# A ranking product ten places behind its logits, and the first expert's gathers three places later

## The chip, the core and the metric

One core of a Trainium2 chip runs the whole program. The metric is the device time of one execution in microseconds (us). TensorE (PE) multiplies matrices, VectorE (DVE) and ScalarE (ACT) work on tiles, GpSimd (POOL) issues the indirect transfers (scatters and gathers by a list of rows), and SyncE (SP) issues the plain transfers. Each engine works through a queue of its own in order, and an instruction that has to wait holds up everything behind it on that engine.

## What is computed

Attention over 4 sequences of 576 tokens with 8 heads and fixed masks; then a gated feed-forward layer; then a mixture of 8 experts of which each token uses two. The core of the reference, with what matters here:

```python
attn = softmax(where(mask, q @ k.T / sqrt(D), -1e9)); x = attn @ v       # 2304 tokens x 512
x = (x @ w_a) * (x @ w_b) @ w_out                                        # 512 -> 1536 -> 512
noisy = x @ w_gate + log1p(exp(x @ w_noise)) * noise                     # 2304 x 8
top2 = argpartition(-noisy, 2, axis=1)[:, :2]
top2_w = exp(l - max(l)) / (sum + 1e-9)                                  # l: the two chosen logits
for e in range(8):
    for k in range(2):
        mask = top2[:, k] == e
        out[mask] += top2_w[mask, k] * (relu(x[mask] @ w1[e]) @ w2[e])
```

## The kernel before

Full-precision products are made of three matmuls on split operands (a high part `...h` and a low part `...l`; the helper is L196 to L198). The feed-forward layer runs over five chunks of tokens: chunks 0 to 3 have 512 tokens each (the first 512 of a sequence), chunk 4 has the 256 tokens that are left. A chunk takes twelve steps f = 0 to 11 of 128 hidden units. A step makes `pa` and `pb` (stage_a), `a` on ACT (L703), the product `a*pb` on DVE (L708), its parts `gh` (ACT, L709) and `gl` (DVE, L710). The products into `po` (stage_b) are made one step later: in step f PE runs `pa` and `pb` of f and then `po` of f - 1. In chunk 4, `pa` and `pb` of one step are 24 matmuls of 256 columns, `po` is 6 of 512 columns.

When a chunk's `po` is complete, its routing follows in the next chunk's steps, in pieces: `finish` is a generator, and each `yield` in it ends a piece. Twice per stage_a and once per stage_b a step calls `point()`, which lets the routing go on by one piece, and the loading of expert weights by one or two. For the fourth chunk (c = 3) the pieces run in chunk 4 from f = 1 on: four times a transposition of 128 rows and their logits (eight pieces), then the routing proper on DVE and ACT (L451 to L478), which ends in `ms`, the two chosen experts of each token as ones and zeros. Some empty pieces later PE makes the ranking product (L485): fourteen small matmuls that count, for each token and expert, the tokens before it. From it DVE makes `sli`, the slot of each token in its expert's list (L491 to L498), and POOL scatters the tokens' numbers and weights into the table in DRAM (L510, eight scatters for a chunk of 512).

The first expert's tokens are fetched during chunk 4's last steps by the generator `first` = fetch(0, [0, 1, 2]): load the table (L757, on SP), gather 128 rows (L763, on POOL) twice, transpose the first of the two on PE (L772) and evacuate it into `x00h`, `x00l`, gather the third, transpose the others. A place in the table that chunk 4 fills begins only behind these three tiles, so they depend on the scatters of chunks 0 to 3 alone. The step at which each `next(first)` stands fixes its place on PE; two gathers may be open at a time.

The expert weights come meanwhile through two stage buffers `st` of 512 KB (L156, on SP), one half of a 1 MB unit each; ACT and DVE convert each half into the high and low part (L159, L160: `w0h`, `w0l` to `w7h`, `w7l`, two conversions of each for a half). A buffer is free for the next load when its conversions are done. Units 0 to 2 and 3 to 5 lie where the feed-forward weights of f = 0 to 3 and f = 4 to 7 were, so they can be converted only after chunk 4 has used those for the last time.

PE's order is the order in which the program is written. The order of the other engines is set by a scheduler when the program is built, from estimated times; it can change around the change, though the code there is the same.

Of the kernel before, what the change touches and what calls it, by code (L numbers as in the profile page):

```python
# [32 lines left out]
def attention_moe_kernel(ctx: ExitStack, tc: tile.TileContext, q, k, v, w_a, w_b, w_out,  # L33
                         w_gate, w_noise, noise, w1, w2, out):
    nc = tc.nc
    B, H, S, D = q.shape
    DM = H * D
    DFF = w_a.shape[1]
    E, _, FE = w1.shape
    CT = 512  # L40
    TL = S - CT
    NCH = B + 1
# [157 lines left out]
    def pt(shape, name="tt"):  # L200
        return psum.tile(shape, F32, name=name, tag="t", bufs=2)
# [219 lines left out]
    def tile_of(c):  # L421

        return (4 * c, 4) if c < B else (4 * B, TL * B // 128)
# [22 lines left out]
    def route(c, lg):  # L446
        T0, J = tile_of(c)
        z = lg[:, :, 8:16]
        t4 = rpool.tile([128, 4, J, 8], F32, name="t4", tag="t4")
        e, w, r, sp = (t4[:, i] for i in range(4))  # L450
        nc.vector.tensor_scalar(r, z, -1.0, None, op0=OP.mult)  # L451
        nc.vector.tensor_tensor(r, r, z, op=OP.max)
        nc.scalar.activation(e, r, AF.Exp, scale=-1.0)
        nc.vector.tensor_scalar(w, e, 1.0, None, op0=OP.add)
        nc.scalar.activation(sp, w, AF.Ln)
        nc.vector.scalar_tensor_tensor(e, w, -1.0, e, op0=OP.add, op1=OP.subtract)
        nc.vector.reciprocal(r, w)
        nc.vector.tensor_mul(e, e, r)
        nc.vector.tensor_sub(sp, sp, e)
        nc.vector.scalar_tensor_tensor(sp, z, 0.0, sp, op0=OP.max, op1=OP.add)  # L460
        nc.vector.tensor_mul(sp, sp, noise_sb[:, T0:T0 + J, :])
        nc.vector.tensor_add(sp, sp, lg[:, :, 0:8])
        m8 = rpool.tile([128, J, 8], F32, name="m8", tag="m8")
        i8 = rpool.tile([128, J, 8], U32, name="i8", tag="i8")
        for j in range(J):
            nc.vector.max(m8[:, j, :], sp[:, j, :])
            nc.vector.max_index(i8[:, j, :], m8[:, j, :], sp[:, j, :])
        wt = rpool.tile([128, 2, J], F32, name="wt", tag="wt")
        nc.vector.tensor_sub(wt[:, 1, :], m8[:, :, 1], m8[:, :, 0])
        nc.scalar.activation(wt[:, 1, :], wt[:, 1, :], AF.Exp)  # L470
        idf = rpool.tile([128, J, 2], F32, name="idf", tag="idf")
        nc.vector.tensor_copy(idf, i8[:, :, 0:2])
        oh = rpool.tile([128, J, 2, 8], F32, name="oh", tag="oh")
        for j in range(J):
            nc.vector.tensor_tensor(oh[:, j], iota8[:, None, :].to_broadcast([128, 2, 8]),
                                    idf[:, j, :, None].to_broadcast([128, 2, 8]), op=OP.is_equal)
        ms = rpool.tile([128, J, 8], BF, name="ms", tag="ms")
        nc.vector.tensor_add(ms, oh[:, :, 0, :], oh[:, :, 1, :])  # L478
        yield
        yield  # L480
        yield
        rk = pt([128, J + 1, 8])
        for j in range(J + 1):
            for jj in range(min(j, J - 1) + 1):
                nc.tensor.matmul(rk[:, j, :], tri if jj == j else ones, ms[:, jj, :],  # L485
                                 start=(jj == 0), stop=(jj == min(j, J - 1)))
        if c == NCH - 1:
            for e in range(2):
                nc.vector.tensor_scalar(base[:, e:e + 1], base[:, e:e + 1], float(e * NT + GAP), None, op0=OP.max)
        sl = rpool.tile([128, J, 8], F32, name="sl", tag="sl")  # L490
        nc.vector.tensor_add(sl, rk[:, 0:J, :], base[:, None, :].to_broadcast([128, J, 8]))  # L491
        nc.vector.tensor_add(base, base, rk[:, J, :])
        for kk in range(2):
            nc.vector.tensor_mul(oh[:, :, kk, :], oh[:, :, kk, :], sl)
        slf = rpool.tile([128, 2 * J], F32, name="slf", tag="slf")
        nc.vector.tensor_reduce(slf, oh.rearrange("p j k e -> p (j k) e"), axis=AX.X, op=OP.add)
        sli = rpool.tile([128, 2 * J], I32, name="sli", tag="sli", bufs=2)
        nc.vector.tensor_copy(sli, slf)  # L498
        pay = rpool.tile([128, J, 2, 2], I32, name="pay", tag="pay", bufs=2)
        for kk in range(2):  # L500
            nc.vector.tensor_copy(pay[:, :, kk, 0], ids[:, T0:T0 + J])
        payf = pay.bitcast(F32)
        den = rpool.tile([128, J], F32, name="den", tag="den")
        nc.vector.tensor_scalar(den, wt[:, 1, :], 1.0, 1e-9, op0=OP.add, op1=OP.add)
        nc.vector.reciprocal(den, den)
        nc.vector.tensor_copy(payf[:, :, 0, 1], den)
        nc.vector.tensor_mul(payf[:, :, 1, 1], wt[:, 1, :], den)
        for j in range(J):
            for kk in range(2):
                ins = nc.gpsimd.indirect_dma_start(  # L510
                    out=table, out_offset=bass.IndirectOffsetOnAxis(ap=sli[:, 2 * j + kk:2 * j + kk + 1], axis=0),
                    in_=pay[:, j, kk, :], in_offset=None)
                for o in scatters:
                    tc.declare_no_dep(ins.ins, o.ins, reason="every slot is written once")
                scatters.append(ins)
        yield
# [20 lines left out]
    bgq, attq, finq = [], [], []  # L537

    def advance(queue):
        while queue:  # L540
            try:
                next(queue[0])
                queue.append(queue.pop(0))
                return
            except StopIteration:
                queue.pop(0)
# [5 lines left out]
    def drain():  # L552
        while bgq or finq:
            pump()
# [75 lines left out]
    def conv_to(n):  # L630

        while nconv[0] < n:
            nconv[0] += 1
            if behind[0] is None:
                next(conv)
            else:
                with tc.issue_after(behind[0].ins):
                    next(conv)
# [151 lines left out]
    with tc.manual_schedule(engines={mybir.EngineType.PE}):  # L790
        first = fetch(0, [0, 1, 2])
        prev = None
        npt = [0]
        for c, f in ORDER:
            n0, n1 = nconv[0], min(48, 12 + 3 * (f + 1) if f < 8 else 36 + 6 * (f - 7))

            def point():
                npt[0] += 1
                if c == 0:
                    conv_to(n0 + (n1 - n0) * ((npt[0] - 1) % 3 + 1) // 3)  # L800
                advance(attq)
                advance(finq if finq else attq)
                advance(bgq)
                if c == NCH - 1:
                    advance(bgq)

            if c == 0 and f == 8:
                conv_to(36)
                last_units(cp, 10, ("u0", "u1", "u2"))
                conv_room["raw"] = halves(rpool, [128, 512, 2], "raw", "row")  # L810
                conv_room["ct"] = lambda m: rpool.tile([128, 512], I32, name="ct", tag="x2T")
            if f == NF - 1:
                while c + 1 < B and (c + 1, HPS[-1]) not in attended:
                    advance(attq)
                if c == 0:
                    conv_to(48)
            if c == 1 and f == 0:
                late_setup()
            if (c, f) == (B - 1, 0):
                bgq.append(clear_out())  # L820
                att.close()
                xr = ctx.enter_context(tc.tile_pool(name="xr", bufs=1, side="right"))
                xpool[0, 0] = xr
                xpool["g"] = xr
            if (c, f) == (B - 1, 2):
                for kd in HPS:
                    xf[B, kd] = mpool.tile([128, TL * B], F32, name="xf", tag="xf", bufs=4)
                    nc.sync.dma_start(xf[B, kd], tails[:, kd, :])
            if (c, f) == (NCH - 1, 4):
                bgq.append(load_expert(0))  # L830
            if c == NCH - 1 and f in (8, 11):
                for _ in range(3 if f == 8 else 2):
                    next(first)
            g = stage_a(c, f, point)
            if f == NF - 1 and c + 1 < NCH:
                for kd in HPS:
                    split_kd(c + 1, kd)
                may[0] = c + 2
            if prev is not None:
                rows = stage_b(*prev, point)  # L840
                if rows is not None:
                    finq.append(finish(prev[0], rows))
            prev = (c, f, g)
        drain()
        last_rows = stage_b(*prev, pump)
        for _ in first:
            pass
# [175 lines left out]
```

## Time and profile before

| | |
|---|---|
| median of 3 runs | 1141.54 us (1140.45 to 1141.98) |
| profiled execution | 1142.42 us |
| its span, first to last instruction | 1140.6 us |
| mean granted TensorE clock | 0.961 of 2.4 GHz |
| PE busy | 1097.2 us, 96% |
| DVE, ACT, POOL busy | 511.5, 432.3, 141.8 us |
| longest wait of PE for another engine | 6.9 us, product L485 for `ms` |

The profile tells for each instruction when it started, how long it ran and, where its engine had been idle before it, what ended that wait. PE's matmuls overlap, so the distance from one start to the next tells more than the length of one. The granted clock has two levels, 1.00 (2.4 GHz) and 0.50 (1.2 GHz); a number between them is a mean over a stretch.

### The profile page before, as it was taken

What the parts mean: (1) busy time and instruction counts of PE and PEld (TensorE: products, weight loads), DVE (VectorE), ACT (ScalarE), POOL (GpSimd) and SP (SyncE); (2) the same over time, 40 slices, a digit from 0 to 9 for tenths busy, and PEclk for the clock granted to TensorE, in tenths of its full rate; (3) what the DMA queues carried; (4) which work ended last, traced back from release to release, by engine and by line L of the source; (5) the groups of instructions that cost most, each with busy time, mean ns of one, the idle gap of its engine ahead of it and who ended that gap; (6) DMA issues with size and microseconds to landing.
All of it is one profiled execution on the core that took longest, in us unless ns stands there. A gap on an engine that the chain in (4) does not pass through costs nothing.

```text
span 1140.6 us, 16116 instructions
## 1 busy us (share of the span) xinstructions
PE 1097.2 (96%) x6411; PEld 929.8 (82%) x6411; DVE 511.5 (45%) x1075; ACT 432.3 (38%) x935; POOL 141.8 (12%) x136
## 2 busy tenths in 40 slices
PE   6989999999999999999997899989999999999996
PEld 4767777887778877888887799978999999999995
DVE  5849777735545444323135552245343334342211
ACT  4767877422333322212124532244242324241110
POOL 0000000002000020002002123221121313131111
PEclk7579999999999999999998999998999999999998
DMA  9535434200212021900003434266254635442123
GB/s 187 131 99 169 144 109 144 79 22 13 57 37 70 12 53 41 330 29 2 1 37 111 151 109 75 43 194 172 83 121 119 129 112 121 120 122 37 21 29 47
DMA packets 88549, 105.02 MB, mean 92 GB/s; under 512 B 43664, under 2 KB 48400, under 8 KB 88464
## 3 DMA queue, kind: packets, MB, share of 16 engines
q1 hardware_dynamic: 78352, 82.89, 24.5%
q0 software_dynamic: 10112, 21.02, 10.2%
q8 instruction: 52, 0.85, 0.3%
q14 instruction: 33, 0.27, 0.1%
HBM read 78.53 MB, written 25.35 MB: 91 GB/s over the span
## 4 chain that ended last, share of the span: by engine, by line
PE 81%; DVE 7%; DMA 6%; ACT 3%; issue 1%; another core or an unknown queue 1%; SPq 1%; POOL 0%; ACTq 0%; POOLq 0%; DVEq 0%
PE ph L196 6%; PE ph L198 6%; PE ph L197 6%; PE py L196 6%; PE py L197 6%; PE py L198 6%; PE pa L196 4%; PE pb L196 4%; PE po L196 4%; PE pb L197 4%; PE pb L198 4%; PE pa L197 4%; PE pa L198 4%; PE po L198 4%; PE po L197 4%; PE tt L290 2%
## 5 line engine op out<-in xcount | busy, mean ns | idle before, releaser
L873 DVE SCALAR_TENSOR_TENSOR hl<-ph,hh 128x256 fp32r<-128x256 f32 (+1 forms) x128 | 62.3, 489 | 213.9 <-ACT hh L872 212.6
L872 ACT ACTIVATE hh<-ph 128x256 fp32r<-128x256 f32 (+1 forms) x128 | 55.2, 433 | 225.0 <-PE ph L198 222.5
L708 DVE TENSOR_TENSOR a<-a,pb 128x512 f32<-128x512 f32 (+1 forms) x60 | 37.9, 632 | 130.5 <-PE pb L198 124.8
L897 POOL DMA_INDIRECT out_dram<-y,tb x40 | 64.0, 1600 | 185.7 <-ACT y L896 144.8
L510 POOL DMA_INDIRECT table<-pay,sli x36 | 35.1, 975 | 411.3 <-DVE sli L498 384.2
L703 ACT ACTIVATE a<-pa 128x512 f32<-128x512 f32 (+1 forms) x60 | 33.1, 551 | 120.4 <-PE pa L198 118.2
L763 POOL DMA_INDIRECT g<-x,tb x40 | 40.1, 1003 | 192.1 <-PE tt L772 170.0
L709 ACT ACTIVATE gh<-a 128x512 fp32r<-128x512 f32 (+1 forms) x60 | 35.1, 586 | 70.7 <-DVE a L708 57.2
L710 DVE TENSOR_TENSOR gl<-a,gh 128x512 fp32r<-128x512 f32 (+1 forms) x60 | 38.1, 635 | 20.0 <-ACT gh L709 18.8
L290 PEld LDWEIGHTS tt<-kT,qT 64*72 64x72 f32 (+1 forms) x336 | 29.5, 149 | 13.4 <-issue 10.3
L290 PE MATMUL tt<-kT,qT 64*72 64x72 f32 (+1 forms) x336 | 37.6, 253 | 1.1 <-ACT pT L336 1.1
L196 PE MATMUL py<-w6h,hh 128*128 128x512 f32 x80 | 32.3, 406 | 4.0 <-ACT hh L872 4.0
L336 ACT ACTIVATE pT<-tt 128x288 f32<-128x288 f32 (+1 forms) x64 | 24.9, 408 | 28.7 <-PE tt L335 28.7
L196 PE MATMUL pa<-xh,w0h 128*128 128x512 f32 (+1 forms) x80 | 32.7, 408 | 1.6 <-ACT xh L414 1.4
L335 PE MATMUL tt<-ident,s 72*72 72x72 f32 (+1 forms) x224 | 29.4, 263 | 4.2 <-DVE s L327 2.1
L335 PEld LDWEIGHTS tt<-ident,s 72*72 72x72 f32 (+1 forms) x224 | 22.3, 140 | 12.6 <-ACT qT L262 2.9
L196 PE MATMUL pb<-xh,w4h 128*128 128x512 f32 (+1 forms) x80 | 31.5, 394 | 0.6 <-issue 0.6
L197 PE MATMUL py<-w6l,hh 128*128 128x512 f32 x80 | 32.0, 400 | 0.0
L196 PE MATMUL pb<-xh,w1h 128*128 128x512 f32 (+1 forms) x80 | 31.9, 399 | 0.0
L196 PE MATMUL py<-w3h,hh 128*128 128x512 f32 x80 | 31.8, 398 | 0.0
L196 PE MATMUL py<-w2h,hh 128*128 128x512 f32 x80 | 31.8, 399 | 0.0
L196 PE MATMUL pa<-xh,w3h 128*128 128x512 f32 (+1 forms) x80 | 31.6, 395 | 0.0
(294 smaller groups left out, 3283.6 us busy)
## 6 DMA issues: line engine op xcount, KB each, us to landing
st<-in_moe_w_dram SPq DMA_DIRECT2D x64, 512.0 KB
out_dram<-zero SPq DMA_DIRECT2D x13, 512.0 KB
raw<-in_moe_w_a_dram SPq DMA_DIRECT2D x4, 1024.0 KB
raw<-in_moe_w_b_dram SPq DMA_DIRECT2D x4, 1024.0 KB
raw<-in_moe_w_out_dram SPq DMA_DIRECT2D x4, 1024.0 KB
x<-row SPq DMA_DIRECT2D x16, 256.0 KB
raw<-in_moe_w_a_dram SPq DMA_DIRECT2D x4, 512.0 KB
raw<-in_moe_w_b_dram SPq DMA_DIRECT2D x4, 512.0 KB
```

Source lines behind the costliest of these rows:

```text
L196: nc.tensor.matmul(ps, w[0], x[0], start=start, stop=False)
L197: nc.tensor.matmul(ps, w[0], x[1], start=False, stop=False)
L198: nc.tensor.matmul(ps, w[1], x[0], start=False, stop=stop)
L290: nc.tensor.matmul(ps[:, ii, :], self.qT[r0:r0 + 64, q0:q0 + n], self.kT[r0:r0 + 64, k0:k0 + m], start=not pemask, stop=not pemask or ii = ...
L335: nc.tensor.transpose(ps[:, ii, :], self.s[half][:, x, ii, :], ident[:n, :n])
L510: ins = nc.gpsimd.indirect_dma_start(out=table, out_offset=bass.IndirectOffsetOnAxis(ap=sli[:, 2 * j + kk:2 * j + kk + 1], axis=0), in_=pa ...
L708: nc.vector.tensor_mul(a, a, pb)
L710: behind[0] = nc.vector.tensor_sub(gl, a, gh.bitcast(F32))
L763: nc.gpsimd.indirect_dma_start(out=g, out_offset=None, in_=x2, in_offset=bass.IndirectOffsetOnAxis(ap=TB[e, t][:, 0:1], axis=0))
L872: nc.scalar.activation(hh, ph, AF.Relu)
L873: nc.vector.scalar_tensor_tensor(hl, ph, 0.0, hh.bitcast(F32), op0=OP.max, op1=OP.subtract)
L897: ins = nc.gpsimd.indirect_dma_start(out=out, out_offset=bass.IndirectOffsetOnAxis(ap=TB[e, t][:, 0:1], axis=0), in_=y, in_offset=None, co ...
```

## The change

The routing of the fourth chunk has ten empty pieces between `ms` and the ranking product instead of three; the other chunks keep three. The first three pieces of `first` (the table load and two gathers) stand at f = 9 instead of f = 8 of chunk 4, a step and so three calls of `point()` later, and what is left of the routing is run out before them (at f = 9 and at f = 11, where the two next pieces still stand). No computation is added or removed.

```diff
         nc.vector.tensor_add(ms, oh[:, :, 0, :], oh[:, :, 1, :])
-        yield
-        yield
-        yield
+        for _ in range(10 if c == B - 1 else 3):
+            yield
         rk = pt([128, J + 1, 8])
...
-            if c == NCH - 1 and f in (8, 11):
-                for _ in range(3 if f == 8 else 2):
+            if c == NCH - 1 and f in (9, 11):
+                while finq:
+                    advance(finq)
+                for _ in range(3 if f == 9 else 2):
                     next(first)
```

On PE the fourteen matmuls of the fourth chunk's product move (`tt` is the product, `tri` and `ones` its constant weights). Before, they stand at the end of step f = 4 of chunk 4, between `po` of f = 3 (weights w2) and `pa` of f = 5 (weights w3):

```order
L197 MATMUL po<-w2l,gh 128x512
L198 MATMUL po<-w2h,gl 128x512
L485 LDWEIGHTS tri
L485 MATMUL tt<-ms,tri 128x8
L485 LDWEIGHTS ones
L485 MATMUL tt<-ms,ones 128x8
...
L196 MATMUL pa<-xh,w3h 128x256
```

In the changed kernel (its lines here are one lower) they stand in step f = 7, between `pa` (w3) and `pb` (w4):

```order
L197 MATMUL pa<-xl,w3h 128x256
L198 MATMUL pa<-xh,w3l 128x256
L484 LDWEIGHTS tri
L484 MATMUL tt<-ms,tri 128x8
L484 LDWEIGHTS ones
L484 MATMUL tt<-ms,ones 128x8
...
L196 MATMUL pb<-xh,w4h 128x256
```

What moved is the product alone, by two steps and a `pa`, 72 matmuls further back; PE's other instructions keep their order.

On DVE, the queue from `ms` to `sli` before, where the conversions of the third unit (w2l) are the only ones between:

```order
L478 TENSOR_TENSOR ms<-oh 128x32
L160 TENSOR_TENSOR w2l<-st,w2h 128x512
L505 RECIPROCAL den<-den 128x4
L160 TENSOR_TENSOR w2l<-st,w2h 128x512
L491 TENSOR_TENSOR sl<-tt,base 128x32
...
L496 TENSOR_REDUCE slf<-oh 128x8
L498 CAST sli<-slf 128x8
L708 TENSOR_TENSOR a<-a,pb 128x256
```

The changed kernel's queue from the first use of the product (`sl`) to `sli`:

```order
L490 TENSOR_TENSOR sl<-tt,base 128x32
L160 TENSOR_TENSOR w3l<-st,w3h 128x512
L491 TENSOR_TENSOR base<-base,tt 128x8
L493 TENSOR_TENSOR oh<-oh,sl 128x4x8 x2
L160 TENSOR_TENSOR w3l<-st,w3h 128x512
...
L495 TENSOR_REDUCE slf<-oh 128x8
L707 TENSOR_TENSOR a<-a,pb 128x256
L160 TENSOR_TENSOR w3l<-st,w3h 128x512 x2
L497 CAST sli<-slf 128x8
```

Here `sli` now stands behind all four conversions of the fourth unit (w3l) and behind `a` of f = 7; before, those came after it.

On SP, the queue after the stores of the fourth chunk's rows (`st` are the loads of expert weights, `tb` the table, two loads of it side by side, `x_57<-row` the stores of rows), before:

```order
L529 DMA x_57<-row 128x512 x8
L156 DMA st<-in_moe_w_dram 128x2x512 x6
L757 DMA tb<-table 128x6 x2
L156 DMA st<-in_moe_w_dram 128x2x512 x6
L533 DMA x_57<-row 64x512 x4
```

and in the changed kernel:

```order
L528 DMA x_57<-row 128x512 x8
L156 DMA st<-in_moe_w_dram 128x2x512 x12
L756 DMA tb<-table 128x6 x2
L532 DMA x_57<-row 64x512 x4
```

The table load moved behind six more loads of weights. Two loads of `st` stand further ahead in both queues, so these six are the third to the eighth, and the six that are now ahead of the table are the ninth to the fourteenth.

## Rows read from the trace of the kernel before

**Rows 1.** The page, first part: busy us (share of the span), instructions.

```profile
PE 1097.2 (96%) x6411; PEld 929.8 (82%) x6411; DVE 511.5 (45%) x1075; ACT 432.3 (38%) x935; POOL 141.8 (12%) x136
```

**Rows 2.** Who waited for whom, PE, 605 to 662: us in total, times, longest.

```profile
PE tt L485 <- DVE ms L478: 6.9, 1, 6.9
...
PE pa L196 <- ACT a L703: 0.5, 2, 0.3
```

**Rows 3.** PE in order of time: start us, us, instruction [idle before <- releaser].

```profile
608.93 0.40 PE L198 MATMUL po<-w2h,gl 128*128 128x512 f32 x1
616.18 0.19 PE L485 MATMUL tt<-ms,tri 128*128 128x8 bf16 x1 [6.86 <-DVE ms L478]
...
616.58 0.56 PE L196 MATMUL pa<-xh,w3h 128*128 128x256 f32 x1
...
623.30 0.28 PE L196 MATMUL pa<-xh,w3h 128*128 128x256 f32 x1
...
627.52 0.28 PE L196 MATMUL pa<-xh,w3h 128*128 128x256 f32 x1
...
646.30 0.60 PE L772 MATMUL tt<-ident,g 128*128 128x128 f32 x4
...
656.20 1.01 PE L196 MATMUL ph<-x00h,w0h 128*128 128x384 f32 x2 [2.16 <-ACT x00h L773]
```

**Rows 4.** Windows: length, busy us of each engine, granted PE clock, DMA share, GB/s.

```profile
616.00:622.00 6.00, 5.82 (x39) 5.82 (x40) 2.42 (x15) 1.50 (x3) 2.16 (x3) 0.50 0.64 178
...
656.00:659.50 3.50, 3.30 (x12) 3.04 (x13) 1.50 (x3) 0.74 (x2) 1.13 (x2) 0.52 0.84 270
```

**Rows 5.** DVE in order of time.

```profile
612.17 0.42 DVE L710 TENSOR_TENSOR gl<-a,gh 128x256 fp32r<-128x256 f32 x1
...
615.94 0.18 DVE L478 TENSOR_TENSOR ms<-oh 128x32 bf16<-128x32 f32 x1
...
618.78 0.17 DVE L498 CAST sli<-slf 128x8 int32<-128x8 f32 x1
```

**Rows 6.** POOL in order of time: first and last scatter, two gathers.

```profile
619.23 0.97 POOL L510 DMA_INDIRECT table<-pay,sli  x1 [84.13 <-DVE sli L498]
...
628.14 0.96 POOL L510 DMA_INDIRECT table<-pay,sli  x1 [0.30 <-issue]
...
647.17 1.38 POOL L763 DMA_INDIRECT g<-x,tb  x1 [10.35 <-PE tt L772]
...
688.61 0.98 POOL L763 DMA_INDIRECT g<-x,tb  x1 [4.29 <-DMA tb<-table]
```

**Rows 7.** SP's issues in order of time.

```profile
618.01 0.37 SPq L156 DMA_DIRECT2D st<-in_moe_w_dram  x1
630.80 0.82 SPq L757 DMA_DIRECT2D tb<-table  x2
632.66 0.38 SPq L156 DMA_DIRECT2D st<-in_moe_w_dram  x1
634.20 0.38 SPq L156 DMA_DIRECT2D st<-in_moe_w_dram  x1
638.42 0.37 SPq L156 DMA_DIRECT2D st<-in_moe_w_dram  x1
642.02 0.37 SPq L156 DMA_DIRECT2D st<-in_moe_w_dram  x1
...
647.76 0.37 SPq L156 DMA_DIRECT2D st<-in_moe_w_dram  x1
...
686.05 1.29 SPq L757 DMA_DIRECT2D tb<-table  x3
```

**Rows 8.** ACT in order of time: the conversion that waits for the load of 632.66.

```profile
636.43 1.16 ACT L159 ACTIVATE w4h<-st 128x512 fp32r<-128x512 f32 x2 [1.45 <-DMA st<-in_moe_w_dram]
```

**Rows 9.** Windows, as in rows 4, behind the gather of 688.61.

```profile
690.00:691.50 1.50, 1.50 (x8) 1.24 (x7) 0.52 (x1) 0.00 (x0) 1.20 (x2) 1.00 0.61 175
```

**Rows 10.** Who waited for whom, SP's own queue, 600 to 660.

```profile
SPq L533 <- DMA g<-x,tb: 4.1, 1, 4.1
```

## The prediction

> **What bounds the kernel now.** I read the page's first part, then the list of who waited for whom on PE, then PE, VectorE (DVE), GpSimd (POOL) and SyncE (SP) in order of time around the place that the diff touches. PE works 96% of the span [rows 1], so time can only come from PE's few waits or from stretches in which it runs slowly. Between 605 and 662 us its longest wait is the one that the change aims at: the ranking product (L485) waits 6.9 us for `ms` [rows 2]. In order of time: the last matmul before it starts at 608.93, the product only at 616.18, and the next step's first matmul at 616.58 [rows 3]. The wait has a tail. The granted clock in 616 to 622 is 0.50, the lower of the two levels, after PE has stood still [rows 4], so step f=5 of the fifth chunk lasts from 616.58 to 623.30, 6.72 us, while f=6 (623.30 to 627.52) takes 4.22 [rows 3]: another 2.5 us. Altogether 6.9 + 2.5 = 9.4 us hang on the product's place.
>
> Those 9.4 us are worth their full amount only if nothing else holds PE before the expert stage. The next fixed point in PE's queue is the first transpose of a gathered tile at 646.30 [rows 3]; it needs the first expert's gather, the gather needs the slot table, and the table needs the scatters that follow the ranking product. In the kernel before, that chain had slack.
>
> **The change, part by part.** All times below are on the clock of the profiled execution before, which took 1142.42 us with a span of 1140.60; the median is 1141.54, and I add the difference to the median.
>
> *The product's wait goes.* PE is free at about 609.2 (608.93 plus the spacing of its matmuls). It now goes on with f=5. One small wait appears: `po` of f=4 needs `gl`, which DVE finishes at 612.17 + 0.42 = 612.6 [rows 5], against 612.0 when PE wants it: 0.6 us. So f=6 starts at 609.2 + 4.22 + 0.6 = 614.0, f=7 at 618.2, and the product, now behind f=7's 1.4 us of `pa`, at 619.6. `ms` was ready at 616.1 [rows 5]; two instructions of f=5 of some 0.4 us each now stand before it in DVE's queue, which makes it 617. The product does not wait any more. It costs the same 0.4 us (616.18 to 616.58). f=8 to f=10 follow at 4.22 each, and PE reaches the transposes at 609.2 + 0.6 + 6 x 4.22 + 0.4 = 635.5 instead of 646.30.
>
> *The scatters come later than the product alone says.* Before, `sli` ended at 618.95 [rows 5], 2.4 us after the product. In the new order of DVE, `sli` stands behind all four conversions into w3l. The last two need the eighth weight load, which SP can issue only when its stage buffer is free, at about 618.4 (618.01 before) [rows 7]. The shortest round trip of a stage buffer, from one load to the next into the same buffer, is 632.66 to 638.42, 5.76 us [rows 7]; one of these steps ends with the conversions. So `sli` ends at about 618.4 + 5.8 + 0.2 = 624.4, 4.4 us after the new product. From `sli`'s end to the table load it took 630.80 - 618.95 = 11.85 us before: eight scatters on POOL from 619.23 to 628.14 + 0.97, and 1.7 us until they have landed [rows 6, 7]. The table may be loaded from 624.4 + 11.85 = 636.25.
>
> *The table load moves back in SP's queue.* Before, it stood behind six loads of `st`; now it stands behind twelve, so it also waits until the last of them is issued. The eighth frees its buffer at 624.2, and the tenth, twelfth and fourteenth use that buffer in turn: two round trips from 624.2 to the fourteenth's issue. Trips seen are 5.76 (632.66 to 638.42), 5.74 (642.02 to 647.76) and 7.82 (634.20 to 642.02, with the first two gathers in the traffic) [rows 7]. The gathers are not in the traffic now, so I take 6.1 each, near the short end: 636.4, and the table load at 636.8. The two conditions, 636.25 and 636.8, nearly coincide. What stands behind the table load on SP (four stores of `row`, four more loads) isn't needed before the expert stage.
>
> *From table to transposes.* A table load issued at 686.05 let the gather start at 688.61, 2.56 us later [rows 6, 7]. Here the fourteenth load, 512 KB, has been issued just before it; a load takes 3.77 us from issue (632.66) to the conversion that waits for it (636.43) [rows 7, 8]. I take the table to land behind it, at 636.4 + 3.8 = 640.2, and the gather to start at 640.5; without the queueing it would be 636.8 + 2.6 = 639.4. The Trainium skill, page "DMA: Bandwidth & Descriptors", section "Queues, rings and completion order", says that each DMA engine consumes a ring's descriptors in order, which puts the table behind the fourteenth load; by that rule the sum is the one below, without it 1.1 us less. No run here shows it. A gather started at 688.61 had its 256 KB through by 691.5 (175 GB/s over 1.5 us) [rows 6, 9]: 2.9 us, and some 0.3 more until PE may start. The slow end is the third gather, which started at 647.17 while a load of `st` was under way; SP's store waited 4.1 us for it from 648.13 on [rows 6, 7, 10], which makes 5.1 us. No load of `st` runs beside it now, so I take 3.3: the transposes start at **643.8**. PE stands still from 635.5 to 643.8, for 8.3 us, with `pa` of f=11 and everything else queued behind.
>
> *After the transposes.* PE starts again after a wait longer than the old one. I charge the same 2.5 us for the slow clock; the other slow stretch, 656.0 to 659.5 at 0.52 [rows 4], lasted 3.3 us after PE resumed at 656.20 and cost half of that, 1.65; if it lasts longer, 3.4. The 0.3 us that `pa` of f=11 waited for `a` [rows 2] disappears, since ScalarE (ACT) is ahead by then. The wait of 2.16 us at 656.20 [rows 3] stays: ACT's queue there is unchanged (row, four conversions, two evacuations).
>
> **Sum.** Stretch up to the transposes: 643.8 - 646.3 = -2.5. Wait on `a`: -0.3. Slow clock after the transposes: +2.5 (the old slow stretch is already left out in the first term). Together -0.3 us: **1141.2 us**. The wait moves from the product to the first gather and is paid there.
>
> **The rivals.**
>
> *The gather is in time and the whole wait is gone.* -6.9 - 2.5 - 0.3 = -9.7: 1131.8. For it speaks that the gather's own code was moved back with the scatters. Against it: from the product's start to the gather's landing even the old, unhindered chain takes 616.18 to 630.80, then 2.6 and 3.2, 20.4 us [rows 3, 6, 7]; PE needs only 16 us from 619.6 to 635.5. Chance 0.05.
>
> *The table is not held up and the slow clock is short.* Table load at 636.25, landing in 2.56 us, gather 3.3: transposes at 642.2, 1.6 less; slow clock 1.65 instead of 2.5. -0.3 - 1.6 - 0.85 = -2.75: 1138.8. Chance 0.20.
>
> *Slower: the weight loads ahead of the table run at the slow pace.* If both round trips take 7.82 us, the fourteenth load goes out at 639.8, 3.4 us later, and all behind it with it: +3.1, 1144.6; with the slow gather of 5.1 us as well, 1146.4. It decides from the point at which the fourteenth load is issued after 639.0. For it speaks that eight scatters are in the traffic now; against it that these are small. Chance 0.16.
>
> *The scatters are stretched by the conversions.* The scatters took 0.97 us each with DVE almost idle; a gather started at 647.17 beside conversions took 1.38 [rows 6]. Now they run beside the conversions into w4l and w5l. Eight times 0.41 is 3.3 us: the table may be loaded from 639.6 and lands at 642.1 instead of 640.2, +1.9: 1143.1. The Trainium skill, page "SBUF — State Buffer", section "Who interferes with whom", says that a VectorE instruction with two SBUF inputs contends with a GpSimd instruction that reads SBUF; these conversions have two. The long gather agrees, the many short ones say that it is rare. Chance 0.06.
>
> **How the numbers follow.** My forecast, the wait moved and nothing measurable left, has 0.53. A measurement of this kernel can tell about 0.2% from no change, 2.3 us, so "same" is 1139.3 to 1143.8. Same: 0.53 + 0.06 = 0.59; faster: 0.05 + 0.20 = 0.25; slower: 0.16. The range takes in the second rival down to 1138.4 and the slower one up to 1144.6; outside lie the whole gain (0.05), half of the slower rival (0.08) and a little of the faster one.
>
> **What would show it.** In the changed kernel's profile PE should have no wait at the ranking product, at about 619.6; `sli` should end near 624.4, the scatters run to 634.5, the fourteenth load of `st` go out near 636.4 and the table load directly behind it; PE should wait some 8 us at the first transposes (L772, one line earlier there), until about 644, and run at half the clock after it. The forecast is wrong if that wait is under 5 us or over 11, if the scatters start before 622, or if the product still waits.

## The result, and the profile after

The changed kernel takes 1148.7 us (median of 4 runs, 1146.25 to 1149.5) against 1141.76 us (1140.45 to 1142.64) for the kernel before beside it: ratio 1.0065, 95% interval 1.0036 to 1.0094. It is slower, by more than the 0.2% that a measurement can tell; the forecast was no change, 1141.2 us, with a range up to 1144.6.

The profiled execution is the lowest of the four, 1146.25 us. Its first part, which answers to [rows 1]:

```profile
span 1144.5 us, 16112 instructions
...
PE 1094.3 (96%) x6411; PEld 926.3 (81%) x6411; DVE 510.9 (45%) x1075; ACT 432.6 (38%) x935; POOL 142.7 (12%) x136
```

PE's busy time has not grown; it waits longer. The two traces have to be laid on each other first: `pa` of f = 4 in the fifth chunk, ahead of everything that the change touches, starts at 605.05 before and at 603.63 after, so 1.42 us are added to a time of after to set it beside one of before or of the forecast. From there to the first matmul of the expert stage (`ph`) it takes 51.15 us before and 56.64 after, and from that matmul to the end 484.4 and 484.2. So the change costs 5.5 us in this one place and nothing behind it; the spans differ by -1.4 + 5.5 - 0.2 = 3.9. The medians differ by 6.9 us; the 1.4 us that this place does not account for are less than the four executions of the changed kernel differ among themselves (3.3 us), and stay open.

The waits of PE from 600 to 670 (us in total, times, longest), which answer to [rows 2]:

```profile
PE tt L771 <- DMA g<-x,tb: 12.8, 1, 12.8
PE ph L196 <- ACT x00h L772: 2.2, 1, 2.2
PE po L196 <- ACT gh L708: 1.5, 1, 1.5
```

The 6.9 us at the product are gone, and 12.8 us at the first transposes have come. In order of time (start, us, instruction [idle before <- releaser]), beside [rows 3]:

```profile
617.87 0.18 PE L484 MATMUL tt<-ms,tri 128*128 128x8 bf16 x1
...
635.88 0.59 PE L198 MATMUL po<-w,gl 128*128 128x512 f32 x1
649.28 1.12 PE L771 MATMUL tt<-ident,g 128*128 128x128 f32 x4 [12.81 <-DMA g<-x,tb]
650.05 0.56 PE L196 MATMUL pa<-xh,w 128*128 128x256 f32 x1
...
660.27 0.62 PE L196 MATMUL ph<-x00h,w0h 128*128 128x384 f32 x2 [2.17 <-ACT x00h L772]
```

The product has no wait. PE reaches the transposes at 649.28 - 12.81 = 636.5 and stands until 649.28: this is 12.8 us where the forecast had 8.3, and over the 11 that it had named as a sign of being wrong. From 635.9 to 653.0 the granted clock is the lower one, 0.50, so `pa` of f = 11 (650.05) starts at half speed.

POOL, beside [rows 6]: the scatters, then the first gather.

```profile
623.48 0.97 POOL L509 DMA_INDIRECT table<-pay,sli  x1 [89.80 <-DVE sli L497]
...
626.03 1.46 POOL L509 DMA_INDIRECT table<-pay,sli  x1 [0.30 <-issue]
627.79 1.43 POOL L509 DMA_INDIRECT table<-pay,sli  x1 [0.30 <-issue]
...
633.36 0.97 POOL L509 DMA_INDIRECT table<-pay,sli  x1 [0.30 <-issue]
645.83 0.98 POOL L762 DMA_INDIRECT g<-x,tb  x1 [11.50 <-DMA tb<-table]
```

The list of transfers from 623 to 640 (the last number is the median time in us from issue to landing) shows that the scatters are slow to land; the last of them, issued at 633.36, lands at 639.19, 4.9 us after POOL is done with it:

```profile
table<-pay,sli POOLq DMA_INDIRECT x8, 6.7
```

SP, beside [rows 7]: the tenth to the fourteenth load of `st` and the table load right behind them.

```profile
623.15 0.37 SPq L156 DMA_DIRECT2D st<-in_moe_w_dram  x1
626.68 0.37 SPq L156 DMA_DIRECT2D st<-in_moe_w_dram  x1
629.01 0.37 SPq L156 DMA_DIRECT2D st<-in_moe_w_dram  x1
634.71 0.37 SPq L156 DMA_DIRECT2D st<-in_moe_w_dram  x1
640.22 0.37 SPq L156 DMA_DIRECT2D st<-in_moe_w_dram  x1
640.64 0.94 SPq L756 DMA_DIRECT2D tb<-table  x2
```

The tenth, twelfth and fourteenth use one buffer. The first of these round trips, 623.15 to 629.01, takes 5.86 us, the second, 629.01 to 640.22, takes 11.21. ACT shows why; it converts each load as soon as that has landed:

```profile
632.67 1.15 ACT L159 ACTIVATE w5h<-st 128x512 fp32r<-128x512 f32 x2 [4.22 <-DMA st<-in_moe_w_dram]
...
638.24 1.15 ACT L159 ACTIVATE w5h<-st 128x512 fp32r<-128x512 f32 x2 [4.12 <-DMA st<-in_moe_w_dram]
```

The eleventh load takes 6.0 us (626.68 to 632.67) and the twelfth 9.2 us (629.01 to 638.24), where [rows 7, 8] show 3.77. The tenth, under way beside the first three scatters, still took 3.9 (623.15 to 627.02), so not every load beside scatters is slow. The windows of these stretches (length, busy us of each engine, granted clock, DMA share, GB/s), beside [rows 4]:

```profile
623.00:626.00 3.00, 3.00 (x21) 2.73 (x21) 1.51 (x6) 1.54 (x3) 1.94 (x2) 1.00 0.71 229
626.00:629.00 3.00, 3.00 (x25) 2.87 (x24) 2.30 (x6) 1.84 (x4) 2.67 (x2) 1.00 0.69 51
629.00:632.00 3.00, 3.00 (x24) 2.87 (x23) 0.31 (x1) 0.00 (x0) 2.17 (x3) 1.00 0.84 212
...
635.00:638.00 3.00, 1.40 (x4) 0.67 (x4) 0.02 (x1) 0.00 (x0) 0.00 (x0) 0.65 0.49 14
```

In the second and the fourth of these stretches the DMA engines are taken for 0.69 and 0.49 of the time and move 51 and 14 GB/s; in [rows 4], with a share of 0.64, they moved 178. In the first and the third they move 229 and 212: the slowness comes in stretches. From 635 on POOL has issued all scatters (634.3), but not all have landed, and ACT, DVE and soon PE wait.

### The profile page after: what moved, and what is told of

Read it like the earlier page. It is cut to its first block, busy times and chain, and to the rows that moved or that the text cites. A ratio compares the mean times of both kernels' runs of the same rounds, so it can differ in the third digit from the quotient of the medians.

```text
span 1144.5 us, 16112 instructions
## 1 busy us (share of the span) xinstructions
PE 1094.3 (96%) x6411; PEld 926.3 (81%) x6411; DVE 510.9 (45%) x1075; ACT 432.6 (38%) x935; POOL 142.7 (12%) x136
## 5 line engine op out<-in xcount | busy, mean ns | idle before, releaser
L873 ACT ACTIVATE hh<-ph 128x256 fp32r<-128x256 f32 (+1 forms) x128 | 55.2, 434 | 221.2 <-PE ph L198 221.1
L771 PE MATMUL tt<-ident,g 128*128 128x128 f32 x160 | 25.5, 276 | 13.6 <-DMA g<-x,tb 12.8
L771 PEld LDWEIGHTS tt<-ident,g 128*128 128x128 f32 x160 | 19.9, 142 | 17.6 <-DMA g<-x,tb 13.4
L196 PE MATMUL py<-w7h,hh 128*128 128x512 f32 x80 | 31.5, 394 | 0.0
```

What stands on the lines that cost most here:

```text
L196: nc.tensor.matmul(ps, w[0], x[0], start=start, stop=False)
L771: nc.tensor.transpose(ps[:, kd, :], g[:, 128 * kd:128 * kd + 128], ident)
L873: nc.scalar.activation(hh, ph, AF.Relu)
```

## The experiments

Each kernel ran beside the kernel before on its chip. In the table, times are counted from the start of `pa` of f = 4 in the fifth chunk of the same trace; "table" is the issue of the first table load, "transposes" the first of a gathered tile, "expert" the first `ph`. The ratio is to the kernel before, with its interval. The times come from one traced execution each, the ratio from all: two traces of the same kernel differ by 1.3 us at "expert" (the two held ones with the earlier product), and the trace of the last row is the slowest of its ten executions (1145.22 us, median 1140.69).

| kernel | product | first scatter | table | transposes | expert | ratio |
|---|---|---|---|---|---|---|
| before | 11.1 | 14.2 | 25.8 | 41.3 | 51.2 | 1 |
| the change | 14.2 | 19.9 | 37.0 | 45.7 | 56.6 | 1.0065 (1.0036 to 1.0094) |
| product alone | 14.3 | 20.0 | 36.3 | 44.2 | 55.2 | 1.0042 (1.0022 to 1.0062) |
| gathers alone | 11.1 | 14.2 | 26.4 | 41.2 | 50.7 | 0.9998 (0.9984 to 1.0012) |
| no scatters | 14.1 | none | early | 30.8 | 40.1 | one run |
| loads held | 14.2 | 19.3 | 31.2 | 39.8 | 53.4 | 1.0043 (1.0026 to 1.0060) |
| transposes late | 14.3 | 19.8 | 37.4 | 45.5 | 57.4 | 1.0057 (1.0036 to 1.0077) |
| held and late | 14.9 | 20.3 | 33.6 | 43.7 | 54.9 | 1.0034 (1.0018 to 1.0049) |
| table on GpSimd | 14.2 | 19.7 | 35.7 | 42.3 | 53.7 | 1.0034 (1.0016 to 1.0053) |
| held, earlier product | 11.5 | 14.9 | 27.7 | 35.8 | 48.2 | 0.9956 (0.9935 to 0.9977) |
| the same on another chip | 11.8 | 15.1 | 27.7 | 35.8 | 46.9 | 0.9954 (0.9937 to 0.9971) |
| earlier product, not held | 11.8 | 15.1 | 29.0 | 38.7 | 49.3 | 0.9994 (0.9974 to 1.0014) |
| the same, table on GpSimd | 11.4 | 14.9 | 31.8 | 42.2 | 53.7 | 1.0005 (0.9992 to 1.0018) |

My theory from the result (A): the first gather is late, first because the loads of `st` and the scatters now run at the same time and slow each other, and second because the product stands so late that the chain from it to the gathered tile is longer than what PE has left to do. The rivals: the gathers' own later place, or the loads being slow by themselves.

### The two halves of the change

The product alone keeps the gathers at f = 8; the gathers alone keep the product at three pieces.

```diff
-            if c == NCH - 1 and f in (9, 11):
+            if c == NCH - 1 and f in (8, 11):
...
-                for _ in range(3 if f == 9 else 2):
+                for _ in range(3 if f == 8 else 2):
```

```diff
-        for _ in range(10 if c == B - 1 else 3):
+        for _ in range(3):
```

> The product ten places behind its logits, the gathers left at f=8 and f=11. Theory A (the table load stands behind the ninth to fourteenth weight loads on SP, and these run beside the eight scatters): SP's queue is the same as in the changed kernel (twelve loads, then the table), so the time stays at 1146 to 1149.5 us and PE waits 11 to 14 us at the first transposes. Rival C (the gathers' later place costs the time): back to 1141 to 1143 us.

> The product at its old place, the gathers at f=9 and f=11. SP's queue has six loads and then the table, as before the change. Theory A: 1141 to 1143 us, PE waits 6.9 us at the product again and under 1 us at the first transposes. Rival C (the gathers' later place costs the time): 1146 to 1149 us.

With the product alone PE waits 11.3 us at the transposes and the ratio is 1.0042; its round trips are 5.66 us (625.14 to 630.80) and 10.62 us (630.80 to 641.42). With the gathers alone PE waits 6.8 us at the product as before, not at all at the transposes, and the ratio is 0.9998. The loss comes with the product's place; the gathers' place costs nothing while the product is at its old one. Beside the late product the two ratios with and without it, 1.0065 and 1.0042, have intervals that overlap, so 0.2% for the gathers' place can't be told from nothing there.

### The loads without the scatters

The fourth chunk's eight scatters are left out (the table then lacks that chunk's tokens), and with them what the table load waits for.

```diff
-        for j in range(J):
+        for j in range(J if c != B - 1 else 0):
             for kk in range(2):
                 ins = nc.gpsimd.indirect_dma_start(
```

> The changed kernel without the eight scatters of the fourth chunk (its tokens are missing from the lists, the gathers move as many bytes); the table load then stands ahead of the loads. Theory A: the eleventh and twelfth loads, which took 6.0 and 9.2 us from issue to landing in the changed kernel, take under 4.6 us; no wait of PE above 2 us for a gather; 1132 to 1137 us. Rival D (the loads are slowed by each other and by the conversions, not by the scatters): the eleventh and twelfth still take 6 us or more.

One run, 1131.8 us, where the kernel before had 1139.1 (median, 1136.66 to 1143.53). PE doesn't wait at the product or the transposes. The loads, and a window in the stretch that was worst before:

```profile
623.85 0.37 SPq L156 DMA_DIRECT2D st<-in_moe_w_dram  x1
...
629.57 0.37 SPq L156 DMA_DIRECT2D st<-in_moe_w_dram  x1
...
635.66 0.37 SPq L156 DMA_DIRECT2D st<-in_moe_w_dram  x1
```

```profile
631.00:634.00 3.00, 3.00 (x25) 2.79 (x23) 1.20 (x2) 1.80 (x4) 0.00 (x0) 1.00 0.43 154
```

The round trips of the tenth and twelfth loads are 5.72 and 6.09 us, against 5.86 and 11.21 with the scatters, and a share of 0.43 carries 154 GB/s. The eleventh load takes 4.7 us to its conversion, just over the 4.6 that theory A allowed, and far from the 6 of its rival; the other four stretches of 3 us from 622 to 637 move 167 to 199 GB/s. Scatters beside loads cost the fourteenth load some 5 us. The run also gives a bound for what the change is worth when the first gather is in time: the expert stage starts 11.1 us earlier than in the kernel before. It is an upper bound, since the table load and the first two gathers went out early too, the gathers some 43 us earlier than before.

### The scatters without the loads

The second expert's loads, the ninth and later, are put behind the first table load in SP's queue, where they stood in the kernel before. Only their order changes.

```diff
+    def held(gen):
+        while True:
+            with tc.issue_after(TBI[0].ins):
...
-    bgq.append(load_expert(1))
+    bgq.append(held(load_expert(1)))
```

> The changed kernel with the loads of the second expert's weights (ninth and later) queued behind the first table load on SP. Theory A: the scatters land within 2.5 us of the last issue (5.8 in the changed kernel), the table load goes out near 635 us, PE waits 4 to 7 us at the first transposes instead of 12.8, and the time is 1138.5 to 1142 us. Rival B (the product is simply too late for the gathers, whatever stands on SP): PE still waits over 10 us there and the time stays at 1146 to 1149 us.

The wait at the transposes is 9.4 us, between what the two theories expected, and the ratio stays at 1.0043. What the theory says of the scatters holds. POOL, SP and a window:

```profile
631.84 0.97 POOL L509 DMA_INDIRECT table<-pay,sli  x1 [0.30 <-issue]
```

```profile
634.84 0.34 SPq L767 DMA_DIRECT2D tb<-table  x1
```

```profile
629.00:632.00 3.00, 3.00 (x24) 2.87 (x23) 0.85 (x2) 0.42 (x1) 2.10 (x3) 1.00 0.02 1
```

All eight scatters take about 0.97 us, and 2.0 us after the end of the last (632.81) the table load goes out. The transposes come 1.4 us earlier than in the kernel before, but the expert stage 2.3 us later: the held loads now land after the gather, and ACT, which works in order, has their conversions ahead of `x00h`:

```profile
PE ph L196 <- ACT x00h L783: 3.1, 1, 3.1
```

```profile
654.87 1.15 ACT L159 ACTIVATE w6h<-st 128x512 fp32r<-128x512 f32 x2 [0.81 <-DMA st<-in_moe_w_dram]
655.93 1.06 ACT L783 ACTIVATE x00h<-tt 128x512 fp32r<-128x512 f32 x2
```

So the collision is one part. The rest is the chain: 25.6 us from the product to the transposes even with no load beside the scatters, of which PE can fill 16.2 (25.6 - 9.4). Part of the 25.6 is `sli`, which still stands behind the conversions into w3l: from the product to the first scatter it is 5.1 us here and 3.1 in the kernel before.

### Other repairs at the late product

The transposes behind f = 11, alone and with the loads held:

```diff
-            if c == NCH - 1 and f in (9, 11):
+            if (c, f) == (NCH - 1, 9):
                 while finq:
                     advance(finq)
-                for _ in range(3 if f == 9 else 2):
+                for _ in range(3):
```

> The changed kernel, but the transposes of the first gathered tile are issued behind the chunk's last step (f=11) instead of ahead of it; nothing else moves. In the changed kernel PE stood still for 12.8 us at these transposes while f=11 was queued behind. Theory A (the first gather lands at about 649 because of the loads and scatters ahead of it; PE loses only what it can't fill): f=11 now runs first, its 6.7 us at half clock or 4.2 at full clock fill the wait, the wait at the transposes falls to 7 to 9 us, and the expert stage's first matmul comes 3 to 5 us earlier than the 660.3 of the changed kernel. Time 1141 to 1144, ratio to the kernel before 1.000 to 1.003. Rival B (the stage behind is held by something later than the transposes, the conversions of the gathered tile or the third gather, whose buffer now comes free later): the first matmul of the expert stage or the next one after it stays within 1.5 us of the changed kernel's place, or the wait moves to the third gather's transposes, and the ratio stays at 1.004 to 1.008.

> Both repairs together: the second expert's loads of st (the 9th and later) wait behind the first table load in SP's queue, so that no load runs beside the scatters, and the transposes stand behind f=11. With the loads held alone the gather landed at 643.4 and PE waited 9.4 us from 634 on. Theory A: f=11 fills about 4.2 us at full clock plus what the lower clock cost; the transposes wait 4 to 5 us, the first matmul of the expert stage comes at 651 to 654 instead of 657.0, and the time is 1136.5 to 1140, a ratio to the kernel before of 0.996 to 0.9995. Rival B (what was held back, the 9th to 14th loads, is now missed by the second expert, or the conversions of the gathered tile come behind other work): first matmul after 655.5 or a new wait over 3 us between 657 and 700 that the held kernel didn't have, ratio 1.002 or more.

Neither brings what was expected: 1.0057 and 1.0034. PE with the transposes late:

```profile
642.64 0.58 PE L196 MATMUL pa<-xh,w 128*128 128x256 f32 x1 [3.73 <-ACT a L702]
...
651.66 0.66 PE L771 MATMUL tt<-ident,g 128*128 128x128 f32 x4 [0.48 <-DMA g<-x,tb]
...
661.86 1.09 PE L771 MATMUL tt<-ident,g 128*128 128x128 f32 x4 [8.07 <-DVE w7l L160]
```

Now f = 11 (642.64) is held by `a` of the step before, because ACT stands 4.52 us for the slow load of w5h ahead of it; and the third tile's transposes (661.86) wait 8.07 us. The line puts that down to w7l, but what landed last, at 661.72, is the third gather, which POOL issued only at 658.04. Rival B said just that. In the kernel with both repairs PE waits 5.47 us for `gh` of f = 11, since ACT has a held load's conversion ahead of it (4.91 us of waiting for w4h), and 7.56 us for the third gather. The transposes' place isn't where the time is lost.

The first table load from GpSimd's queue, behind the scatters and no longer behind the loads:

```diff
-        nc.sync.dma_start(tb, table[e * NT + 128 * t0:e * NT + 128 * (t0 + n), :].rearrange("(p t) c -> p t c", t=n))
+        (nc.gpsimd if (e, t0) == (0, 0) else nc.sync).dma_start(tb, table[e * NT + 128 * t0:e * NT + 128 * (t0 + n), :].rearrange("(p t) c -> p t c", t=n))
```

> The changed kernel with one difference: the first expert's table is loaded from GpSimd's queue, behind the scatters, instead of from SP's behind the 12 loads of st. All loads run beside the scatters as in the changed kernel. It tells what of the late gather (table landed 645.0, transposes 649.3) is the place in SP's queue behind the 14th load and what is the slow landing of the scatters (639.2). Theory A (both bind, one 5.8 us behind the other): the table is issued at 639 to 640.5 and lands by 642.5, the transposes start at 644.5 to 646.5, the wait of PE at them falls from 12.8 to 8 to 10 us; time 1142 to 1145.5. Rival B (any small transfer is slow while loads are under way, whichever queue issues it): the table lands at 644 or later again, transposes at 648 or later, time as the changed kernel's, 1146 or more.

```profile
638.74 0.59 POOL L756 DMA_DIRECT2D tb<-table  x1 [6.05 <-DMA table<-pay,sli]
641.89 1.00 POOL L762 DMA_INDIRECT g<-x,tb  x1 [2.56 <-DMA tb<-table]
```

Theory A: the wait falls to 8.6 us, the ratio to 1.0034. The table's way from issue to gather is 3.15 us here (638.74 to 641.89) and 5.19 us in the changed kernel (640.64 to 645.83). But the table still can't go out before 638.74, 6.05 us after the end of the last scatter, against 2.0 with the loads held and 1.7 before [rows 6, 7]. Most of that is the landing: the last scatter ends at 632.69 and lands at 638.11, 5.4 us later; the other 0.6 us pass on GpSimd before the issue (in the kernel with both repairs SP issues the table at 636.44, when the last scatter has landed at 636.42). SP's queue and the slow landing are two barriers one behind the other.

### The product two places earlier

With the loads held, and without (twice, once with the table on GpSimd's queue):

```diff
-        for _ in range(10 if c == B - 1 else 3):
+        for _ in range(8 if c == B - 1 else 3):
```

> The held kernel (second expert's loads behind the first table load) with the ranking product two places earlier (8 yields instead of 10). There the chain from the product to the landed gather took about 25 us against 16 us of PE's work, so PE waited 9.4 us at the transposes. Theory A (the lateness of the product alone is left): the product runs 2 to 3 us earlier, sli, scatters, table and gather with it, PE's wait at the transposes falls to 6.5 to 8 us, transposes at about 641, first matmul of the expert stage 1.5 to 3 us earlier than 657.0; ratio to the kernel before 1.000 to 1.003. Rival B (sli is held by the conversions ahead of it in DVE's queue, not by the product): sli and the scatters start within 1 us of the held kernel's (622.9) although the product is earlier, and the wait stays at 9 us or more.

> The changed kernel with the ranking product two places earlier (8 yields instead of 10), the second expert's loads not held. With the changed kernel (10, not held: 1.0065), the held one (10, held: 1.0043) and the held one with the earlier product (8, held: 0.9956) it fills a table of two by two. In SP's queue the table load now stands behind 9 loads of st instead of 12. Theory A (the product's place decides, the loads only add to it): sli and scatters start where they did in the held kernel with the earlier product, 15 us after the first pa of f=4, the wait of PE at the first transposes is 5 to 8.5 us, ratio 0.995 to 0.9995. Rival B (the loads beside the scatters are what costs; without holding them the earlier product brings nothing): wait of 9 us or more at the transposes and a ratio of 1.002 or more.

> The held kernel with the product at 8 yields once more, on the same chip as the two runs beside it, since the comparison of held and not held rests on differences of a few tenths of a per cent. Theory A (loads beside the scatters still cost something at 8 yields): ratio 0.994 to 0.998 and 0.1 to 0.4% below the run that doesn't hold the loads. Rival B (holding makes no difference once the product is earlier): the two within 0.1%.

> The changed kernel with 8 yields instead of 10 and the first expert's table loaded from GpSimd's queue; the loads of st are not held and run beside the scatters. Theory A (each cause counts for itself: the table's place behind the loads gave 1.0065 to 1.0034 at 10 yields, the product's place 1.0043 to 0.9956 when held): the table is issued as soon as the scatters have landed, PE's wait at the transposes is 4.5 to 7.5 us, ratio 0.993 to 0.998. Rival B (with the product earlier the table no longer stands behind a late load, so the queue makes no difference): table issued and landed within 1 us of the run beside it that has the table on SP, and the same ratio within 0.2%.

Held, it is **faster than both kernels**: 0.9956 on one chip (1135.6 us, 1133.32 to 1138.41, against 1140.01) and 0.9954 on another (1133.94, 1131.38 to 1136.05, against 1139.06). The wait at the transposes is 5.5 and 5.1 us. It gains more than theory A expected, and DVE's queue shows a reason (the second of these runs):

```profile
612.67 0.18 DVE L478 TENSOR_TENSOR ms<-oh 128x32 bf16<-128x32 f32 x1
...
614.60 0.18 DVE L490 TENSOR_TENSOR sl<-tt,base 128x32 f32<-128x32 f32 x1
...
615.81 0.17 DVE L497 CAST sli<-slf 128x8 int32<-128x8 f32 x1
616.88 1.29 DVE L160 TENSOR_TENSOR w3l<-st,w3h 128x512 fp32r<-128x512 f32 x2 [0.90 <-ACT w3h L159]
```

Here `sli` stands ahead of the conversions into w3l. In the changed kernel it comes behind them:

```profile
621.83 1.29 DVE L160 TENSOR_TENSOR w3l<-st,w3h 128x512 fp32r<-128x512 f32 x2 [0.63 <-ACT w3h L159]
623.04 0.17 DVE L497 CAST sli<-slf 128x8 int32<-128x8 f32 x1
```

From the product to `sli`'s start it is 2.9 us (612.91 to 615.81) and 5.2 us (617.87 to 623.04). A product 2.4 to 2.8 us earlier than in the changed kernel brings the scatters forward by 4.7 to 5.0; against the held kernel at ten pieces the scatters come 4.2 to 4.4 earlier and the wait at the transposes falls by 3.9 to 4.3. And it costs PE nothing: `ms` is ready at 612.85 and the product starts at 612.91.

Not held, the earlier product is no faster than the kernel before: 0.9994, at the upper end of what theory A gave, and 0.4% slower than with the loads held on the same chip (the intervals, 0.9974 to 1.0014 and 0.9937 to 0.9971, just don't touch). PE waits only 2.4 us at the transposes, less than expected, but it gets there late: the ninth to eleventh loads are issued ahead of the table again. Two windows and ACT:

```profile
620.00:623.00 3.00, 3.00 (x23) 2.79 (x22) 2.27 (x5) 1.46 (x3) 2.39 (x3) 1.00 0.73 28
...
629.00:632.00 3.00, 3.00 (x20) 2.40 (x19) 1.91 (x4) 0.83 (x3) 0.00 (x0) 1.00 0.71 17
```

```profile
635.38 1.15 ACT L159 ACTIVATE w5h<-st 128x512 fp32r<-128x512 f32 x2 [4.41 <-DMA st<-in_moe_w_dram]
636.44 0.40 ACT L708 ACTIVATE gh<-a 128x256 fp32r<-128x256 f32 x1
```

Shares of 0.73 and 0.71 carry 28 and 17 GB/s (155 and 181 in the two windows between), and the late load reaches PE by another way too: `gh` stands behind the conversion on ACT, and PE waits 2.3 us for it; another 1.5 us of PE's standing still, at 628.4, has no cause that the profile names. The transposes come at 38.7 instead of 35.8. With the table on GpSimd's queue as well the ratio is 1.0005, within 0.2% of the kernel beside it, as rival B said, though not for B's reason: there the table goes out 5.87 us after the end of the last scatter, which in that slow execution is later (31.8) than from SP (29.0). Theory A's 0.993 to 0.998 is missed.

The four kernels make a table of two by two: at ten pieces 1.0065 not held and 1.0043 held, at eight pieces 0.9994 and 0.9955 (mean of two). Eight pieces are worth 0.7 to 0.9%; holding the loads is worth 0.4% at eight, and 0.2% at ten, where the intervals overlap.

## Why the prediction was wrong, point by point

*The product's wait goes*: right. Product at 617.87 + 1.42 = 619.3 (forecast 619.6), without a wait. PE reaches the transposes later than forecast, at 636.5 + 1.42 = 637.9 instead of 635.5: in f = 10 `po` waits 1.5 us for `gh`, which stands behind the conversion of the eleventh load on ACT, and the clock falls at 635.9. This cost nothing, as the gathered tile came later still.

*`sli`, behind the conversions into w3l*: right. It ends at 623.21 + 1.42 = 624.6 (forecast 624.4).

*The scatters*: they end at 634.33 + 1.42 = 635.8 (forecast 634.5); two of the eight took 1.46 and 1.43 us instead of 0.97, the size that the last rival gave to all eight. What was missed is their landing, **the other half of the step that failed**: 1.7 us after the last in the sum, 4.9 us in the changed kernel, at 639.19 + 1.42 = 640.6. So the first of the two conditions for the table load, forecast at 636.25, came 4.4 us late by itself, whatever stood on SP.

*The table load moves back in SP's queue*: **this step failed**, by its term "two round trips of 6.1". The first was 5.86 us, the second 11.21. The price was right for loads alone (5.72 and 6.09 without the scatters); I had read it from stretches with no scatter in them, and I wrote for the rival that eight scatters in the traffic are small. They are small in bytes. So the fourteenth load went out at 640.22 + 1.42 = 641.6 instead of 636.4, 5.2 us late, and the table behind it. Had the trips taken 6.1 us as forecast, the landing would still have held the table until 640.6; the two conditions again nearly coincide, both late for one reason: the scatters and the loads run at the same time.

*From table to transposes*: gather 5.2 us after the table's issue instead of 3.7, so another 1.5 late; gather to transposes 3.45 us (forecast 3.3). That the table comes in behind the fourteenth load agrees with the rule of ring order in the Trainium skill that the prediction cites: 5.19 us behind it, 3.15 on the other queue, though the state of the traffic differed as well. It is not shown by that: in the kernels with the loads held the table goes out ahead of the next load, and still takes 4.4 to 4.7 us to the gather. The transposes are at 649.28 + 1.42 = 650.7 instead of 643.8: 5.2 + 1.5 + 0.15 = 6.9 us late. In place of the first term, -2.5, stands +4.4.

*After the transposes*: +2.5 for the slow clock less 0.3 for `a` was forecast; from the transposes to the first `ph` it grew from 9.90 to 10.99, +1.1, half of the 2.2 forecast. The slow stretch ended 3.7 us after PE resumed, and the wait for `x00h` (2.17) stayed as said. Sum 4.4 + 1.1 = 5.5 instead of -0.3.

*The rivals.* The slower one named the place (the round trips ahead of the table) and the point from which it decides (a fourteenth load after 639.0; it was 641.6), at 1144.6 us. Its reason, that the scatters are in the traffic, was the right one, and I gave it 0.16 because I weighed the scatters by their size. The price of 7.82 us for a trip came from gathers in the traffic, and scatters cost more. A gain of the size of rival one's 9.7 us is there when the gather is done long before: without the scatters the expert stage starts 11.1 us earlier.

A second error lies in what I did with a number that I had. I worked out that the chain from the product to the gathered tile takes 20.4 us unhindered and PE's work 16, and used it against the whole gain alone. It also says that, once the chain is longer than PE's work, each us that the product stands later is a us more of waiting. The runs agree, with DVE's order on top: 2.4 to 2.7 us at the product, 3.9 to 4.3 us at the wait. With the product's place two pieces earlier and the loads held, the kernel is 0.45% faster.

## What to carry to other kernels

Move a consumer back only as far as its input needs: when a long chain hangs on it, every place beyond that is paid at the chain's end, and the scheduler may put other work between (here 2.8 us on PE became 5 us at the scatters). When a reordering brings two kinds of transfers together that used to follow one another, a price read from a stretch with one kind alone is no price for the other; look at what the DMA engines moved while both ran, not at the bytes. A change that loses may hold a gain that one order in a queue gives back: look for the queue that it moved unasked.

## What the runs showed of the hardware that was not expected

The eight scatters of the fourth chunk are 256 packets with 0.01 MB in all (256 of the 257 packets that the trace has from 622.9 to 635 in the kernel with the loads held). Beside 512 KB loads both kinds suffer: a load takes 6.0 and 9.2 us from issue to conversion, 4.1 to 4.7 without scatters; the median scatter lands 6.4 to 6.7 us after its issue in the four kernels with loads beside them whose traces tell it, and 3.0 and 3.2 in two with the loads held:

```profile
table<-pay,sli POOLq DMA_INDIRECT x8, 3.0
```

The line is of the held kernel with the earlier product. The table load went out 1.7 to 2.1 us after the end of the last scatter where no load ran beside it, with one exception (3.25 us, in the kernel with both repairs) that nothing here explains. While both run, there are stretches of 3 us in which engines that are taken for 0.49 to 0.73 of the time move 14 to 51 GB/s, and others with 131 to 229 GB/s; loads alone moved 154 GB/s at 0.43. The Trainium skill, page "DMA: Bandwidth & Descriptors", section "Specifications", says that a transfer below 512 B is made by reading and writing back; the trace counts all 256 packets as below 512 B, but no run shows the reading. The Trainium skill, page "DMA: Bandwidth & Descriptors", section "Back-pressure in remote DMA", says, of transfers between cores, that stalled writes stall an engine's other queues too. The slow loads agree with such a stall, inside one core, but no run here shows which write was stalled, so the cause stays open; that each kind slows the other is shown by taking away the one and the other.
